# Retention of two batches in halves of 64 tokens, every product 64 by 64 by 64

## The chip, the core and the metric

The kernel runs on one core of a Trainium2 chip. The core has TensorE (PE, matrix products; loads of its stationary operand are listed as PEld), VectorE (DVE), ScalarE (ACT), GpSimd (POOL) and SyncE (SP), which issues all DMAs here. PE reads SBUF and writes PSUM, a memory of eight banks of 512 float32 per partition. The metric is the time of one execution on the device in microseconds (us), lower being better.

## The reference, cut to what matters

```python
# q, k, v: (4 batches, 8 heads, 576 tokens, 64), float32
scores = q @ k^T / 8
D[i, j] = gamma_h ** (i - j) if i >= j else 0,   gamma_h = 1 - 2 ** (-5 - h)
ret    = (scores * D) @ v                         # retention: causal, decaying by head
x      = ret with the heads side by side          # (2304 tokens, 512)
h      = ((x @ w1) * (x @ w2)) @ w3 @ w_out       # first block
y      = h @ w_in;  g = max(y, 0) + alpha * min(y, 0);  out = g @ w_out2
```

The retention can be computed by chunks of tokens: within a chunk by scores times decay times v, and against all earlier tokens by a state, the decayed sum of k^T v (64 by 64 per head).

## The kernel before, in words

All of it is one program without loops on the chip; Python writes the instructions out. The order on PE, ScalarE and SyncE is that in which they are written; VectorE's and GpSimd's instructions are placed by a scheduler, which chooses among the ready ones, and each of the two then follows its fixed list.

The retention handles two heads at a time as a pair (four pairs per batch): one head on partitions 0 to 63, one on 64 to 127. The class Retention (line 371) cuts a batch into four chunks of 128 tokens and a tail of 64. Its products, per chunk and pair:

- scores (line 400): k^T q, contraction over 64, output 128 by 128, one product per head, into the tile sc (two banks, one buffer). VectorE multiplies sc by the decay mask into rt (line 423).
- values (line 451): state times q (line 467, 64 by 64, moving 128 tokens) and v times rt (line 476, contraction over 128), both summed in the tile o (one buffer in the batches of this change). ScalarE rounds o to the high half xh of x, VectorE takes the rest as xl (lines 181 and 182, called by parts).
- moments (line 427): k^T v of the chunk (line 434, contraction over 128, output 64 by 64) into st (one buffer). VectorE adds them to the aged state: S (line 442, line 440 in the first chunk); GpSimd multiplies S by gamma ** 128: aged (line 446).

A step (line 496) writes the scores of chunk c + 1, the values of chunk c and the moments of chunk c + 1, so a batch has six steps, c = -1 to 4. What VectorE and ScalarE have to do is put off through the list `later` and written at the next flush.

In the third and fourth batch (crossed, line 363) the heads of odd pairs are swapped between the partition halves, so that state products use all four 64 by 64 quadrants of the PE array; cross (line 516) reloads parts of the constants for it by 16 small DMAs.

Between the steps stands the first block: ab_unit (line 621) writes two groups of 12 products of 128 by 128 by 512 (gemm3, line 188, float32 split in two halves) and after each group calls a function that flushes and, at a given rate, runs the next step. In the third batch a step comes after every second group (rate 7/15), in the fourth mostly after each (rate 7/9). VectorE and ScalarE also prepare weights there: lines 93 to 122 turn the bits of 64-bit weights into float32 (a, b), lines 271 to 309 build sums of them (t, wo2u).

Of the kernel before, what the change touches and what calls it, by code (L numbers as in the profile page):

```python
# [7 lines left out]
F32 = mybir.dt.float32  # L8
# [138 lines left out]
def retention_moe_kernel(ctx: ExitStack, tc, qk, kv, w_out1, w3t, w12, w_in, w_out2, alpha, c_row, c_pair, out):  # L147
# [79 lines left out]
    class Operands:  # L227
# [4 lines left out]
        def __init__(self, rooms, small=None, stays=None):  # L232
            self.rooms, self.small, self.stays, self.turn = rooms, small, stays, 0
            self.w = Weights(nc, None, room, 0)
            for c in range(C2):
                self.w.add(w_out2[c], None)
            self.calls, self.u = {}, {}
            self.now = 0
# [11 lines left out]
        def places(self, j, u):  # L250
            ops = self.PLACES[u]
            if j == self.stays:
                return [wop[4 * WOPS.index(op) + 3][:, 1].rearrange("p (h w) -> p h w", h=2) for op in ops]
            n = len(ops)
            if n == 1 and self.small:
                t = self.small.tile([P, 512], F32R, tag="u1", name=f"wo2{u}_{j}")
            else:
                t = self.tile(f"wo2{u}_{j}").bitcast(F32R)[:, 0:512 * n]
            return t.rearrange("p (n h w) -> p n h w", n=n, h=2)
# [83 lines left out]
    abp = pool(pb, "abp", side="right")  # L343
    per_pair = decay.tile([P, NPAIR, 3 * CH + 64], F32, name="per_pair")
    mask = per_pair[:, :, 0:2 * CH].rearrange("p n (h i) -> p h n i", h=2)
    mtail = per_pair[:, :, 2 * CH:2 * CH + 64]
    qs = per_pair[:, :, 2 * CH + 64:]
    per_row = decay.tile([P, 128], F32, name="per_row")[:, 0:H + NPAIR]
# [22 lines left out]
    class Retention:  # L371
# [28 lines left out]
        def scores(self, c):  # L400
            b, n = self.b, self.n
            sc = self.psum["sc"].tile([P, 2, 512], F32, tag="sc", name=f"sc{b}_{c}")
            q, k = qt[b], kt[b]
            if c == NCH - 1:
                rt = self.rt[c] = attn.tile([P, NPAIR, 64], F32, tag="rte", name=f"rte{b}")[:, 0:n]
                for m, p in enumerate(self.pairs):
                    for rows, _, _ in places(b, p):
                        nc.tensor.matmul(sc[rows, 0, m * 64:(m + 1) * 64], k[p][rows, 512:S],
                                         q[p][rows, 512:S],
                                         start=True, stop=True, skip_group_check=True)  # L410
                later.append(lambda: nc.vector.tensor_tensor(
                    out=rt, in0=sc[:, 0, 0:64 * n].rearrange("p (n i) -> p n i", n=n), in1=mtail[:, self.ps],
                    op=ALU.mult))
                return
            i0 = c * CH
            rt = self.rt[c] = attn.tile([P, 2, NPAIR, CH], F32, tag="rt", name=f"rt{b}_{c}", bufs=2)[:, :, 0:n]
            for m, p in enumerate(self.pairs):
                for rows, _, r in places(b, p):
                    nc.tensor.matmul(sc[:, r, m * CH:(m + 1) * CH], k[p][rows, i0:i0 + CH],  # L419
                                     q[p][rows, i0:i0 + CH],  # L420
                                     start=True, stop=True, skip_group_check=True)

            later.append(lambda: nc.vector.tensor_tensor(
                out=rt, in0=sc[:, :, 0:n * CH].rearrange("p h (n i) -> p h n i", n=n), in1=mask[:, :, self.ps],
                op=ALU.mult))
# [70 lines left out]
        def steps(self):  # L496
# [9 lines left out]
                return run  # L506
            return [step(c) for c in range(-1, NCH)]

    qt, kt, kvt, vt = ({b: {} for b in range(B)} for _ in range(4))

    def in_places(b, p, t, src):

        for rows, pp, _ in places(b, p):
            nc.sync.dma_start(out=t[rows], in_=src[pp])  # L514

    def cross():

        for p in range(1, NPAIR, 2):
            in_places(2, p, gc[:, p:p + 1], c_row[:, H + p:H + p + 1])
            for h in range(2):  # L520
                nc.sync.dma_start(out=mask[:, h, p], in_=c_pair[:, p, (1 - h) * CH:(2 - h) * CH])
            in_places(2, p, mtail[:, p], c_pair[:, p, 2 * CH:2 * CH + 64])
            in_places(2, p, qs[:, p], c_pair[:, p, 2 * CH + 64:])

    def load_pair(b, p):
        x = attn.tile([P, 2, S], F32, tag=f"qk{p}", name=f"qk{b}_{p}")
# [143 lines left out]
        return run  # L670

    def retention(b):
        r = Retention(b, list(range(NPAIR)), psum1)
        left = [p for p in range(NPAIR) if (b, p) not in prepared]

        def prep():
            r.scale(left)
            r.prep(left)

        return Steps([prep] + r.steps())  # L680
# [369 lines left out]
    class Group:  # L1050
# [6 lines left out]
        def product(self, ps, a, b, fresh=True):  # L1057
            a, b = operand(self.j, a), xop[self.p, b]
            n = 0
            for k in range(2):  # L1060
                ks = slice(k * P, (k + 1) * P)
                for x, y in ((0, 0), (0, 1), (1, 0)):
                    nc.tensor.matmul(ps, a[:, x, ks], b[:, y, k], start=(fresh and n == 0), stop=(n == 5),  # L1063
                                     skip_group_check=True)
                    n += 1
# [424 lines left out]
```

## Time and profile before

| | |
|---|---|
| median of three runs | 782.3 us (779.87 to 785.56) |
| the profiled execution | 783.55 us, of which its span 781.7 us |
| PE busy | 768.9 us (98%), 4928 records of products |
| DVE busy | 587.3 us (75%) |
| ACT busy | 380.4 us (49%) |
| POOL busy | 63.8 us (8%) |
| mean granted clock of PE | 0.997 of full speed |

Times in the profile count from the start of the span. "Busy" joins overlapping instructions; products on PE are pipelined and their ends modelled, so the starts say more than the durations. A float32 product appears as two records, each with its weight load.

### The profile page before, as it was taken

The numbers are of one execution on the slowest core, as the hardware profiler recorded it, in microseconds if no ns is written. First come the engines' busy times: TensorE is split into PE (matmuls) and PEld (weight loads), VectorE is DVE, ScalarE is ACT, GpSimd is POOL, SyncE is SP. The second block draws the span as 40 slices with busy tenths as digits, with TensorE's granted clock in tenths as the row PEclk, the third lists the DMA queues.
The fourth block names the chain that finished last, engine by engine and source line by source line (L and its number), as shares of the span: only waits on it lengthen the run. The fifth ranks groups of instructions, "written<-read, shape, count | busy, mean of one in ns | idle before, by whom it ended". The sixth has DMA issues, their size and how long they took to land.

```text
span 781.7 us, 13197 instructions
## 1 busy us (share of the span) xinstructions
PE 768.9 (98%) x4928; PEld 688.9 (88%) x4928; DVE 587.3 (75%) x951; ACT 380.4 (49%) x665; POOL 63.8 (8%) x73
## 2 busy tenths in 40 slices
PE   8999999998999999999999999999999999999998
PEld 5788788887788988899999999999999888888887
DVE  4894889569857779688974768778767877777874
ACT  3643474334445466464654546546534444444442
POOL 4410400051000000000000200110200000000000
PEclk9999999999999999999999999999999999999999
DMA  9943965798576667799993796564899754444440
GB/s 353 358 160 105 340 246 202 239 287 259 212 249 204 189 197 256 248 327 368 407 375 138 262 362 225 172 228 154 286 339 366 234 152 128 140 126 136 135 128 28
DMA packets 116225, 182.11 MB, mean 233 GB/s; under 512 B 9920, under 2 KB 82624, under 8 KB 116160
## 3 DMA queue, kind: packets, MB, share of 16 engines
q1 hardware_dynamic: 116160, 181.26, 68.1%
q8 instruction: 39, 0.64, 0.4%
q14 instruction: 26, 0.21, 0.1%
HBM read 117.00 MB, written 64.23 MB: 232 GB/s over the span
## 4 chain that ended last, share of the span: by engine, by line
PE 83%; DVE 7%; DMA 5%; issue 2%; SPq 2%; ACT 1%; POOL 0%; DVEq 0%; ACTq 0%; POOLq 0%
PE h L1063 21%; PE ps L188 19%; PE y L1007 13%; PE o L1208 12%; PE o L1210 6%; PE pw L822 6%; DMA abd<-ab 2%; PE sc L419 2%; PE o L476 2%; DMA cells<-gd 2%; DVE cells L1189 2%; PE o L467 1%; SPq L514 1%; PE st L434 1%; DVE a L108 1%
## 5 line engine op out<-in xcount | busy, mean ns | idle before, releaser
L188 PE MATMUL ps<-xh,w 128*128 128x512 f32 (+1 forms) x640 | 186.1, 372 | 1.8 <-ACT f L651 1.8
L188 PEld LDWEIGHTS ps<-xh,w 128*128 128x128 f32 x640 | 116.1, 188 | 23.3 <-ACT f L651 2.2
L1208 PE MATMUL o<-wop,cells 128*128 128x512 f32 x504 | 126.4, 393 | 0.9 <-DVE cells L1220 0.9
L188 PE MATMUL ps<-xl,w 128*128 128x512 f32 (+1 forms) x320 | 118.0, 369 | 0.0
L1208 PEld LDWEIGHTS o<-wop,cells 128*128 128x128 f32 x504 | 90.8, 189 | 17.7 <-issue 1.4
L1007 PE MATMUL y<-yab,wp 128*128 128x384 f32 x576 | 100.0, 334 | 0.0
L1007 PEld LDWEIGHTS y<-yab,wp 128*128 128x128 f32 x576 | 99.9, 188 | 0.1
L1189 DVE TENSOR_TENSOR cells<-cells,cells 128x1024 fp32r<-128x1024 f32 x63 | 76.4, 1222 | 25.7 <-ACT cells L1183 25.6
L1210 PEld LDWEIGHTS o<-wop,cells 128*128 128x128 f32 x504 | 68.7, 190 | 4.9
L1210 PE MATMUL o<-wop,cells 128*128 128x256 f32 x504 | 70.2, 282 | 0.0
L188 PEld LDWEIGHTS ps<-xl,w 128*128 128x128 f32 x320 | 60.4, 189 | 9.5
L1183 ACT CAST cells<-cells 128x1024 fp32r<-128x1024 f32 x63 | 64.9, 1054 | 7.0 <-DVE cells L1176 4.6
L108 DVE CUSTOM_DVE_ANT_0 a<-a,b 128x1024 uint16<-128x1024 uint16 x72 | 53.2, 738 | 2.9
L1063 PE MATMUL h<-xT,wu 128*128 128x384 f32 x288 | 54.7, 334 | 0.2 <-DVE g L1082 0.2
L1063 PE MATMUL h<-xT,wv 128*128 128x384 f32 x288 | 54.9, 335 | 0.0
L1076 DVE SCALAR_TENSOR_TENSOR g<-h,al,g 128x384 f32<-128x384 f32 x48 | 29.4, 614 | 32.6 <-ACT g L1075 29.5
L637 ACT CAST ab<-f 128x512 fp32r<-128x512 f32 (+1 forms) x40 | 23.1, 577 | 61.2 <-DVE f L641 51.8
L1063 PEld LDWEIGHTS h<-xT,wu 128*128 128x128 f32 x288 | 50.3, 188 | 0.5 <-DVE g L1082 0.5
L1063 PEld LDWEIGHTS h<-xT,wv 128*128 128x128 f32 x288 | 50.3, 188 | 0.3 <-DVE g L1082 0.3
L103 DVE TENSOR_SCALAR a<-a 128x512 f32<-128x512 f32 x72 | 31.9, 443 | 22.9 <-ACT a L93 22.5
L822 PE MATMUL pw<-wo,w 128*128 128x512 f32 x192 | 43.7, 389 | 0.0
L822 PEld LDWEIGHTS pw<-wo,w 128*128 128x128 f32 x192 | 36.0, 188 | 7.4
(130 smaller groups left out, 1139.4 us busy)
## 6 DMA issues: line engine op xcount, KB each, us to landing
gd<-g SPq DMA_DIRECT2D x96, 192.0 KB, 4.4
cells<-gd SPq DMA_DIRECT2D x36, 512.0 KB, 6.3
abd<-ab SPq DMA_DIRECT2D x32, 512.0 KB, 5.2
wod<-wo2u SPq DMA_DIRECT2D x49, 256.0 KB, 4.0
wop<-wod SPq DMA_DIRECT2D x21, 512.0 KB, 6.5
yab<-abd SPq DMA_DIRECT2D x24, 384.0 KB, 8.0
raw<-in_w_dram SPq DMA_DIRECT2D x16, 512.0 KB, 8.0
rawo<-in_w_out_dram SPq DMA_DIRECT2D x16, 512.0 KB, 5.2
```

The source lines that it names most:

```text
L103: nc.vector.tensor_scalar(out=a, in0=a, scalar1=self.LEAST, scalar2=self.MOST, op0=ALU.max, op1=ALU.min)
L108: nc.vector.tensor_tensor(out=a.bitcast(I32), in0=a.bitcast(I32), in1=b, op=ALU.add)
L188: nc.tensor.matmul(ps, a, bb, start=(n == 0), stop=(n == last))
L637: nc.scalar.copy(t[:, 0], f)
L822: nc.tensor.matmul(acc[i], a[:, ic], bb, start=(k == 0 and n == 0), stop=(k == C1 - 1 and n == 2))
L1007: nc.tensor.matmul(ys[o], wpc[c][a][:, oc], yab[b, c][:, bb], start=(c == 0 and i == 0), stop=(c == C1 - 1 and i == 2))
L1063: nc.tensor.matmul(ps, a[:, x, ks], b[:, y, k], start=(fresh and n == 0), stop=(n == 5), skip_group_check=True)
L1076: nc.vector.scalar_tensor_tensor(out=g, in0=ps, scalar=sal[:, c], in1=g, op0=ALU.mult, op1=ALU.max)
L1183: nc.scalar.copy(h.bitcast(F32R), self.q[name])
L1189: nc.vector.tensor_tensor(out=l.bitcast(F32R), in0=q[name], in1=h, op=ALU.subtract)
L1208: nc.tensor.matmul(ps, h[:, k], w[k], start=(fresh and k == 0), stop=(k == C1 - 1), skip_group_check=True)
L1210: nc.tensor.matmul(ps[:, 256:], l[:, k], w[k][:, 0:256], start=False, stop=(k == C1 - 1), skip_group_check=True)
```

## The change

A class Halves takes the place of Retention in the crossed batches. A chunk still has 128 tokens, but its products are of one shape: contraction over 64, 64 columns of output partitions, 64 moving tokens. For scores, only the two diagonal blocks of 64 tokens are made; the decay within a chunk from its first to its second half goes through the state: moments are taken per half, `half` (line 573 or 575) is the state after the first half, S the state after the second. The moments of the first half lie in bank 0 of the tile sc, those of the second in st. A value tile gets v times rt by halves, then, behind a drain of PE, the reads of S for the first 64 tokens and of half for the second, in two groups by the heads' places; the moments (or the tail's scores) of the next chunk are written ahead of each drain. The first 64 rows of the key decay (kd) are replaced by a copy from the mask, and the constants are reloaded in the places that the halves need. In excerpt:

```diff
+    class Halves(Retention):
...
+        def scores(self, c):
...
+            for m, p in enumerate(self.pairs):
+                for rows, _, r in places(b, p):
+                    for h in range(2):
+                        i0 = c * CH + 64 * h
+                        nc.tensor.matmul(sc[HEADS[h], r, m * 64:(m + 1) * 64], k[p][rows, i0:i0 + 64],
+                                         q[p][rows, i0:i0 + 64],
+                                         start=True, stop=True, skip_group_check=True)
+            later.append(lambda: nc.vector.tensor_tensor(
+                out=rt, in0=sc[:, :, 0:64 * n].rearrange("p r (n i) -> p r n i", n=n), in1=mask2[:, :, self.ps],
+                op=ALU.mult))
...
+        def moments(self, c):
...
+            st = [self.sc[:, 0, 256:256 + 64 * n]]
+            st.append(self.psum["st"].tile([P, NPAIR, D], F32, tag="st", name=f"st{b}_{c}")
+                      .rearrange("p n d -> p (n d)")[:, 0:64 * n])
+            def share(m, p):
+                x = None
+                for j, (rows, _, _) in enumerate(places(b, p)):
+                    for h in range(2):
+                        y = nc.tensor.matmul(at[h][rows, m * 64:(m + 1) * 64], v[p][HEADS[h], 4 * j + c],
+                                             v[p][HEADS[h], 8 + 4 * j + c],
+                                             start=True, stop=True, skip_group_check=True)
...
+            def halfway():
+                new = self.half[c] = attn.tile([P, NPAIR, D], F32, tag="half", name=f"half{b}_{c}", bufs=3)[:, 0:n]
+                if c == 0:
+                    nc.vector.tensor_copy(new, st[0])
+                else:
+                    nc.vector.tensor_tensor(out=new, in0=self.state[c], in1=st[0], op=ALU.add)
+                aged = attn.tile([P, NPAIR, D], F32, tag="aged", name=f"aged{b}_{c}", bufs=2)[:, 0:n]
+                nc.gpsimd.tensor_tensor(out=aged, in0=new, in1=gc[:, self.ps].unsqueeze(2)
+                                        .to_broadcast([P, n, D]), op=ALU.mult)
+                def state():
+                    s = self.state[c + 1] = attn.tile([P, NPAIR, D], F32, tag="S", name=f"S{b}_{c}",
+                                                      bufs=3)[:, 0:n]
+                    nc.vector.tensor_tensor(out=s, in0=aged, in1=st[1], op=ALU.add)
+                later.append(state)
+            later.append(halfway)
...
+        def values(self, c, between):
...
+            for m, p in pairs:
+                for h in range(2):
+                    for j, (_, pp, r) in enumerate(places(b, p)):
+                        product(h, pp, m, v[p][HEADS[h], 8 + 4 * j + c], rt[HEADS[h], r, m], False)
+            kinds = 2 if crossed(b) else 1
+            for kind in range(kinds):
+                for x in between[n // kinds * kind:n // kinds * (kind + 1)]:
+                    x()
+                nc.tensor.drain()
+                for h in range(2):
+                    for m, p in pairs:
+                        if kinds == 1 or (p + h) % 2 == kind:
+                            read(m, p, h)
...
+        def steps(self):
+            def step(c):
+                def run():
+                    flush()
+                    if c == NCH - 1:
+                        self.tail_values(c)
+                        return
+                    between = self.scores(c + 1) or self.moments(c + 1)
+                    if c >= 0:
+                        self.values(c, between)
...
     def cross():
+        first_half = HEADS[0]
+        nc.vector.tensor_copy(kd[first_half].rearrange("p (n h) -> p n h", h=2),
+                              mask[first_half, :, :, CH - 1].rearrange("p h n -> p n h"))
...
-        r = Retention(b, list(range(NPAIR)), psum1)
+        r = (Halves if crossed(b) else Retention)(b, list(range(NPAIR)), psum1)
```

How the order moves, at three places. The first is PE in step c = 1 of the third batch (names carry batch and chunk; two equal rows joined as x2, x4). Before, 32 products of four shapes:

```order
L419 MATMUL sc2_2_1446<-qk2_0_916 128x128 x2
L419 MATMUL sc2_2_1446<-qk2_1_938 128x128 x2
...
L467 MATMUL o2_1_1456<-qk2_0_916,S2_0_1312 64x128 x2
L467 MATMUL o2_1_1456<-qk2_1_938,S2_0_1312 64x128 x2
...
L476 MATMUL o2_1_1456<-rt2_1_1351,kv2_0_917 64x128 x2
...
L434 MATMUL st2_2_1473<-kv2_0_917 64x64 x2
```

and now 64 products of one shape:

```order
L541 MATMUL sc2_2_1501<-qk2_0_917 64x64 x4
...
L617 MATMUL o2_1_1520<-rt2_1_1370,kv2_0_918 64x64 x4
...
L562 MATMUL sc2_2_1501<-kv2_0_918 64x64
L562 MATMUL st2_2_1519<-kv2_0_918 64x64
...
L617 MATMUL o2_1_1520<-qk2_0_917,S2_0_1364 64x64 x2
L617 MATMUL o2_1_1520<-qk2_2_963,S2_0_1364 64x64 x2
L617 MATMUL o2_1_1520<-qk2_1_939,half2_1_1467 64x64 x2
L617 MATMUL o2_1_1520<-qk2_3_992,half2_1_1467 64x64 x2
L562 MATMUL sc2_2_1501<-kv2_2_964 64x64
...
L617 MATMUL o2_1_1520<-qk2_1_939,S2_0_1364 64x64 x2
```

The reads of the state (S, half) have moved from ahead of the products with rt to behind them, in two groups between the moments; a drain, which the order does not list, stands ahead of each group.

The second place is VectorE at the first chunk of the fourth batch (a6, a7 are weights being prepared). Before:

```order
L275 TENSOR_TENSOR wo2u4_2_2023<-t3_2_1981,wo2u4_2_2023 128x2x256
L103 TENSOR_SCALAR a6_2028<-a6_2028 128x512
L423 TENSOR_TENSOR rt3_0_2005<-sc3_0_2004,per_pair_101 128x1024
L104 TENSOR_SCALAR a6_2028<-a6_2028 128x512
L440 COPY S3_0_2057<-st3_0_2014 128x256
```

and now:

```order
L275 TENSOR_TENSOR wo2u4_2_2186<-t3_2_2128,wo2u4_2_2186 128x2x256
L103 TENSOR_SCALAR a6_2191<-a6_2191 128x512
L104 TENSOR_SCALAR a6_2191<-a6_2191 128x512
L545 TENSOR_TENSOR rt3_0_2152<-sc3_0_2151,per_pair_101 128x8x64
L573 COPY half3_0_2220<-sc3_0_2151 128x256
L103 TENSOR_SCALAR a7_2195<-a7_2195 128x512
L106 SCALAR_TENSOR_TENSOR a6_2191<-rawo6_2092,a6_2191 128x512
L104 TENSOR_SCALAR a7_2195<-a7_2195 128x512
L583 TENSOR_TENSOR S3_0_2225<-aged3_0_2222,st3_0_2169 128x256
```

L104 has moved ahead of rt, half follows rt, and S, which now needs the aged half, comes four places later.

The third place is VectorE ahead of step c = 3 of the fourth batch, where the last xl of step 2 (two pieces, since a block of x ends within the chunk) frees the output tile. Before:

```order
L275 TENSOR_TENSOR wo2u4_3_2259<-t3_3_2194,wo2u4_3_2259 128x2x256
L103 TENSOR_SCALAR a8_2264<-a8_2264 128x512
L423 TENSOR_TENSOR rt3_3_2224<-sc3_3_2223,per_pair_101 128x1024
L104 TENSOR_SCALAR a8_2264<-a8_2264 128x512
L103 TENSOR_SCALAR a9_2268<-a9_2268 128x512
L106 SCALAR_TENSOR_TENSOR a8_2264<-rawo8_2132,a8_2264 128x512
L104 TENSOR_SCALAR a9_2268<-a9_2268 128x512
L182 TENSOR_TENSOR xl3_1704<-o3_2_2233,xh3_1703 128x4x64
L442 TENSOR_TENSOR S3_3_2297<-aged3_2_2218,st3_3_2250 128x256
L108 ISA a8_2264<-a8_2264,b8_2265 128x1024
L106 SCALAR_TENSOR_TENSOR a9_2268<-rawo9_2134,a9_2268 128x512
L182 TENSOR_TENSOR xl4_2294<-o3_2_2233,xh4_2293 128x4x64
```

and now:

```order
L275 TENSOR_TENSOR wo2u4_3_2530<-t3_3_2429,wo2u4_3_2530 128x2x256
L103 TENSOR_SCALAR a8_2535<-a8_2535 128x512
...
L106 SCALAR_TENSOR_TENSOR a9_2539<-rawo9_2333,a9_2539 128x512
L545 TENSOR_TENSOR rt3_3_2461<-sc3_3_2460,per_pair_101 128x8x64
L575 TENSOR_TENSOR half3_3_2562<-S3_2_2458,sc3_3_2460 128x256
L309 TENSOR_SCALAR a8_2535<-a8_2535,al_71 128x512
L108 ISA a9_2539<-a9_2539,b9_2540 128x1024
L182 TENSOR_TENSOR xl3_1851<-o3_2_2479,xh3_1850 128x4x64
L290 TENSOR_TENSOR t1_4_2674<-a8_2535 128x256
L583 TENSOR_TENSOR S3_3_2573<-aged3_3_2564,st3_3_2478 128x256
L309 TENSOR_SCALAR a9_2539<-a9_2539,al_71 128x512
L182 TENSOR_TENSOR xl4_2569<-o3_2_2479,xh4_2568 128x4x64
```

The five rows left out here are L104, L103, L106, L104 and L108 of a8 and a9. All the preparation of a8 and a9 up to L106 now stands ahead of rt, and 15 instructions instead of 10 lie between wo2u4 and the last xl.

## Rows read from the trace of the kernel before

**Rows 1.** Page, part 1: busy time, share of the span, instructions.

```profile
PE 768.9 (98%) x4928; PEld 688.9 (88%) x4928; DVE 587.3 (75%) x951; ACT 380.4 (49%) x665; POOL 63.8 (8%) x73
```

**Rows 2.** Stretches: length, busy of PE, PEld, DVE, ACT, POOL (instructions), clock, DMA, GB/s.

```profile
175.50:211.40 35.90, 32.77 (x361) 26.51 (x360) 32.72 (x64) 15.64 (x30) 3.72 (x4) 0.95 0.68 236
182.70:186.81 4.11, 4.11 (x48) 3.82 (x48) 4.11 (x10) 0.62 (x1) 2.20 (x1) 0.60 0.98 385
211.40:781.70 570.30, 565.40 (x3189) 527.36 (x3182) 427.00 (x663) 284.82 (x481) 17.09 (x18) 1.00 0.67 226
```

**Rows 3.** Waits of PE, whole span: us in total, times, longest us.

```profile
PE sc L419 <- DVE rt L423: 2.4, 1, 2.4
PE o L467 <- DVE xl L182: 0.6, 1, 0.6
```

**Rows 4.** Chain of waits, third batch: start us, us, what; between them the steps.

```profile
95.34 11.17 PE ps L188 x48
...
108.22 5.69 PE ps L188 x24
...
116.49 5.69 PE ps L188 x24
...
125.35 5.66 PE ps L188 x24
...
134.19 5.66 PE ps L188 x24
...
141.93 5.67 PE ps L188 x24
...
148.22 16.56 PE ps L188 x72
```

**Rows 5.** Timeline of PE in 147.847 to 147.86, last step: start us, us, instruction.

```profile
147.63 0.35 PE L467 MATMUL o<-qk,S 64*64 64x64 f32 x12
147.81 0.24 PE L476 MATMUL o<-rte,kv 64*64 64x64 f32 x4
```

**Rows 6.** Timeline of PE, step c = 3 of the third batch.

```profile
140.19 0.33 PE L467 MATMUL o<-qk,S 64*64 64x128 f32 x2
140.24 0.22 PE L408 MATMUL sc<-qk 64*64 64x64 f32 x2
```

**Rows 7.** Timeline of all engines at the first chunks of the fourth batch.

```profile
181.10 0.42 DVE L103 TENSOR_SCALAR a<-a 128x512 f32<-128x512 f32 x1
181.43 1.21 DVE L423 TENSOR_TENSOR rt<-sc,per_pair 128x1024 f32<-128x1024 f32 x1
...
182.70 2.08 PE L419 MATMUL sc<-qk 64*128 64x128 f32 x16 [2.38 <-DVE rt L423]
...
183.46 2.20 POOL L446 TENSOR_TENSOR aged<-S,per_row 128x256 f32<-128x256 f32 x1 [7.84 <-DVE S L440]
...
186.81 0.50 PE L188 MATMUL ps<-xh,w 128*128 128x512 f32 x1
```

**Rows 8.** Timeline of PE and DVE, steps c = 2 and 3 of the fourth batch.

```profile
198.60 1.16 PE L419 MATMUL sc<-qk 64*128 64x128 f32 x16
...
199.89 0.69 DVE L275 TENSOR_TENSOR wo2u<-t,wo2u 128x512 fp32r<-128x512 f32 x1 [2.12 <-ACT wo2u L271]
200.50 0.42 DVE L103 TENSOR_SCALAR a<-a 128x512 f32<-128x512 f32 x1
...
205.44 0.42 DVE L182 TENSOR_TENSOR xl<-o,xh 128x256 fp32r<-128x256 f32 x1
205.77 0.49 DVE L309 TENSOR_SCALAR a<-a,al 128x512 f32<-128x512 f32 x1
...
206.01 0.67 PE L467 MATMUL o<-qk,S 64*64 64x128 f32 x16 [0.61 <-DVE xl L182]
...
207.63 0.50 PE L188 MATMUL ps<-xh,w 128*128 128x512 f32 x1
```

**Rows 9.** Timeline of SyncE, reloading of the constants ahead of the third batch.

```profile
64.74 2.39 SPq L514 DMA_DIRECT2D per_pair<-const_pair_dram  x4
```

More of the change, by code (lines that the diff above doesn't have):

```diff
@@ L345, in retention_moe_kernel @@
     mask = per_pair[:, :, 0:2 * CH].rearrange("p n (h i) -> p h n i", h=2)
+    mask2 = per_pair[:, :, 0:CH].rearrange("p n (h i) -> p h n i", h=2)
     mtail = per_pair[:, :, 2 * CH:2 * CH + 64]
@@ L516, in cross @@
     def cross():
+        first_half = HEADS[0]
+        nc.vector.tensor_copy(kd[first_half].rearrange("p (n h) -> p n h", h=2),
+                              mask[first_half, :, :, CH - 1].rearrange("p h n -> p n h"))
+        odd = slice(1, NPAIR, 2)
+        for h, rows in enumerate(HEADS):
+            i0 = 64 * h
+            for p in range(0, NPAIR, 2):
+                nc.sync.dma_start(out=per_pair[rows, p, 0:CH].rearrange("p (r i) -> p r i", r=2),
+                                  in_=c_pair[rows, p, 0:2 * CH].rearrange("p (r i) -> p r i", r=2)[:, :, i0:i0 + 64])
+            for r in range(2):
+                at = (1 - r) * CH + i0
+                nc.sync.dma_start(out=per_pair[rows, odd, 64 * r:64 * r + 64], in_=c_pair[rows, odd, at:at + 64])
+        in_places(2, 1, mtail[:, odd], c_pair[:, odd, 2 * CH:2 * CH + 64])
+        in_places(2, 1, qs[:, odd], c_pair[:, odd, 2 * CH + 64:])
         for p in range(1, NPAIR, 2):
             in_places(2, p, gc[:, p:p + 1], c_row[:, H + p:H + p + 1])
[L520 to L523, printed above, removed]
     def load_pair(b, p):
```

77 lines of the change are left out of this document (added).

## The prediction

> **What bounds the kernel now.** I read the page first: TensorE (PE) is busy 98% of the span [rows 1], so the first question for any edit is what it does on PE. Then two stretches: in 175.50 to 211.40, where the fourth batch runs, PE is busy 32.77 of 35.90 us and the granted clock averages 0.95; after it PE is busy 565.40 of 570.30 us [rows 2], so a microsecond won or lost by PE before 211 reaches the end nearly whole. The waits of PE name what makes it idle there: 2.4 us for the decayed scores (rt) and 0.6 us for xl, the low half of an output [rows 3]. Then the chain of waits through batch three: it is PE alone, and the holes between its stretches of L188 are the six steps of the retention [rows 4]: 1.71, 2.58, 3.17, 3.18, 2.08 and 0.62 us (the first begins at 95.34 + 11.17 = 106.51), 13.34 us in all. Batch four has the same products plus its stalls.
>
> **The products.** A float32 product leaves two records on PE. A batch had 288 records in its six steps (32, 48, 64, 64, 48, 32); with every product cut into 64 by 64 by 64 it has 544 (64, 112, 128, 128, 80, 32), as the loops give it: per 128 tokens and pair four products instead of two in scores, in the products with v, in the moments and in the reads of the state, but none more in the last step of 64 tokens. What a 64 by 64 by 64 record costs, the last step shows, where all four quadrants of the array are in turn: 12 records from 147.63 to 147.81, 0.18 us [rows 5], so a round of four takes 0.06. That step's 32 records are 8 rounds, 0.48 of its 0.62 us; 0.14 is entering and leaving.
>
> The new products go round the four quadrants too, except the reads, which come as four products on two quadrants and then four on the other two, and the last scores, on two. PE fills idle quadrants from further down its list: two records of L467 start at 140.19, before the last two of L408 at 140.24 [rows 6]. So I add one round per group of reads and two for the last scores: 16, 30, 34, 34, 24 and 8 rounds.
>
> **The drains.** Steps of 128 tokens now contain two nc.tensor.drain() each, 8 in a batch; no row of these stages shows one. Lower bound: one round, 0.06 us, if the list just goes on. Upper bound from rows: a record lasts 0.22 [rows 6], and PE follows a releaser after 0.06 (rt ends at 181.43 + 1.21 = 182.64, PE starts at 182.70 [rows 7]) to 0.15 (xl ends at 205.44 + 0.42 = 205.86, PE starts at 206.01 [rows 8]): 0.37. An end of a record and a short release are nearest to what a drain says: 0.22 + 0.06 + 0.02 for a refilled array, **0.30**.
>
> Steps of batch three, changed: 0.14 + 16 x 0.06 = 1.10; 0.14 + 1.80 + 0.60 = 2.54; 0.14 + 2.04 + 0.60 = 2.78 twice; 0.14 + 1.44 + 0.60 = 2.18; 0.62. Sum 12.00 against 13.34: **1.3 us gained** (3.3 with drains of 0.06, 0.8 with 0.37). I look for a new wait in it: per chunk VectorE had rt of 1.21 [rows 7] and a narrow S, 0.33, and has rt at half the width, about 0.60, with half and S at 0.33 each, hardly other work in all: 1.54 before, 1.26 now; 24 matmuls of L188 (5.7 us) lie between two steps, and by the order the xl that the next step waits for stays ahead of it. None. GpSimd's fourth ageing per batch has the same cover.
>
> **Batch four, first two steps.** Only 12 matmuls lie between steps (5.66 / 2 = 2.83 us) and VectorE is late. The gain of the first step (0.6) only lets PE wait earlier. In step 0 PE waits for the single buffer of scores. It was free when rt had read it, at 182.64. Now the first half's moments lie in the same buffer, and half must have read it too; and the order puts the second shift (L104) ahead of rt. From L103 at 181.10 [rows 7]: L104 needs its result, 0.42 + 0.04; rt 0.33 later, at 181.90; half 0.60 later, at 182.50; it ends at 182.92 and PE goes on at 182.98 instead of 182.70, +0.28. The wait grows from 2.4 to some 3.2 us. The step took 4.11 us (to 186.81 [rows 7]) where batch three needs 2.58, since after its 2.4 us of idleness PE was granted 0.60 on average, most of it the lower level of 1.2 GHz [rows 2]: 1.5 us lost, which I leave as it is. The second half's moments need S of the first chunk, which now comes behind half and GpSimd's ageing (it took 2.20 us here [rows 7]): S is ready between 184.2 and 185.6, PE needs it at about 184.9, 0 to 0.7, take 0.25. Sum: **0.5 later**. Steps 1 and 2 gain 0.39 each as in batch three: **0.8 earlier**.
>
> **Batch four, step 3.** Here lies the largest term. The outputs have one buffer; the products of step 3 wait for the last xl of step 2. Before, 10 instructions stand on VectorE between wo2u4 (199.89) and that xl; PE starts on the outputs at 206.01, 0.61 late. The new order puts 15 there (the parts of the last weights go ahead of rt, half and xl), and the wait now stands ahead of the step's scores too. By spacing in the rows [rows 8]: a 512-wide instruction 0.61 (199.89 to 200.50), a narrow one 0.33 (205.44 to 205.77), L309 0.49 less the same overlap of 0.09. From wo2u4: six wide ones 3.66, a dependent L103 0.46, seven narrow ones 2.31, two L309 0.80, the last xl 0.42: 7.65. It ends at 207.54 instead of 205.86, and PE starts 0.15 later, at 207.69. wo2u4 itself waits for ScalarE's cast behind the L188 products ahead of step 2, so its distance from step 2 stays. From there the step has 2.18 us to go, against 207.63 - 206.01 = 1.62: it ends at 209.87, **2.2 later**. PE will have idled from about 204.2 (198.60 + 2.78 + 2.83) to 207.7, 3.5 us, more than the 2.4 us after which the clock was lower; a lower clock again costs between 0 and 1.5, take **1.0**.
>
> **The rest.** SyncE issues 16 small transfers where it issued 16, at about 0.6 us each [rows 9], before and behind the same neighbours: nothing, at most 0.5 either way. VectorE's one copy of 64 by 8 at the start of batch two: under 0.2, beside PE's products.
>
> **Sum.** -1.3 + 0.5 - 0.8 + 2.2 + 1.0 = +1.6 us. The profiled execution took 783.55 us, so 785.15; it lies 1.25 above the median of 782.3, so against the median **783.9 us**.
>
> One rule of the Trainium skill speaks against the change. The rows give 15 ns from record to record over 12 records [rows 5], and none shows more than 32 such records in a row. "TensorE: Matmul & The Clock Gate", section "Wait — 56ns, not 53.3ns?", states a floor of about 25 ns from start to start however small a matmul is, and 62 ns if each goes through the sequencer's code. By the floor alone 544 records would be an estimated 13.6 us before any drain, and a batch would lose instead of gain; the rows contradict it over the length they show.
>
> **Rivals.**
> 1. *Drains are cheap and the clock stays up* (faster). Place: 14 drains that count (8 in batch three, 6 in batch four behind its first wait). Below 0.18 us each the sum turns negative: 1.6 - 14 x 0.12 = -0.1. At 0.06 it is 1.6 - 14 x 0.24 = -1.8, and without the second fall of the clock -2.8: 779.5. For it: between the two kinds of products of the last step PE shows no pause [rows 5]; against it: PE is told to empty. 22%.
> 2. *PE cannot sustain the small records* (slower). If a long run of 64 or more goes at 25 ns, half of the 50 at which the 64 records of a step go now (3.17 / 64 [rows 4]), because the list is fed no faster, batch three costs 544 x 0.010 = 5.4 more, batch four 4.8 more after its first wait (480 records): 783.9 + 10.2 = 794. It decides from 18 ns on (544 x 0.003 = 1.6 us a batch). For it: four instructions per product, twice as many products; against it: 12 records at 15 ns, steadily. The same rise comes if a drain costs 0.9. 9%.
> 3. *The wait of step 3 moves the fourth batch further* (slower): VectorE waits for GpSimd's ageing at each S, and the wait repeats in step 4, with the clock down in both: another 3 to 5 us, 787 to 789. For it: the ageing of 2.20 [rows 7]; against it: VectorE has less to do in each step, and ahead of wo2u4 it stood idle for 2.12 us [rows 8]. 14%.
> 4. *The change is not what it says*: the two quadrants of the reads are not filled ahead; 28 rounds a batch rather than 8 extra: 20 x 0.06 = 1.2 us more each, 786.3. Inside my range; 10%.
>
> My forecast as worked out, 782 to 786: 45%.
>
> **Numbers.** A measurement of this kernel can tell about 1% from no change (7.8 us); the runs before lie between 779.87 and 785.56. The range takes in rivals 1, 3 and 4 and the bounds of the drain, and the scatter of a median: 778.5 to 789.5. Faster by over 1% would be under 774.5, more than all gains together: 3%. Slower by over 1% is above 790.1, rival 2 and the end of rival 3: 11%. Within 1%: 86%.
>
> **What would show it.** In the changed profile: the holes between the stretches of L188 in batch three at 1.1, 2.5, 2.8, 2.8, 2.2 and 0.6 us; gaps of 0.3 ahead of the reads, at a record named DRAIN; PE's longest waits 3.2 us for half (L573) and about 3.4 us for xl ahead of step 3 of batch four, the granted clock below 1 in both. I am wrong if PE's small records stand 20 ns or more apart within a group, if VectorE's xl of step 2 does not end some 7.7 us after wo2u4, or if a stretch after 212 gains idle time.

## The result and the profile after

The changed kernel takes 791.2 us, median of 4 runs (789.8 to 794.6), against 782.2 before: the ratio is 1.0126, 95% interval 1.0095 to 1.0156. It is slower by 1.3%; 783.9 was forecast, and 789.5 was the top of the range. The profiled execution took 792.2 us (span 790.4, against 781.7 before). Three executions among all runs of this document took 1.5 to 2.7 ms for no reason that is known and are left out of its medians and ratios.

Part 1 of the page of the changed kernel, as [rows 1], and three views of its trace. The stretches first (columns as in [rows 2]); the first is the fourth batch and the second all that follows, as there:

```profile
PE 769.5 (97%) x5440; PEld 688.1 (87%) x5440; DVE 588.1 (74%) x960; ACT 379.7 (48%) x665; POOL 68.2 (9%) x75
```

```profile
175.50:218.57 43.07, 34.71 (x616) 27.75 (x606) 32.73 (x68) 15.37 (x30) 3.70 (x5) 0.80 0.57 203
218.57:790.40 571.83, 565.65 (x3189) 527.04 (x3182) 426.59 (x663) 284.22 (x482) 17.09 (x18) 1.00 0.67 225
...
182.00:192.00 10.00, 8.69 (x122) 7.37 (x123) 10.00 (x22) 2.06 (x4) 1.66 (x2) 0.50 0.68 236
192.25:209.00 16.75, 14.17 (x295) 11.03 (x293) 10.92 (x22) 6.47 (x12) 1.82 (x2) 1.00 0.53 200
209.25:215.75 6.50, 4.92 (x84) 4.18 (x85) 4.87 (x12) 1.65 (x4) 0.00 (x0) 0.50 0.24 94
```

The fourth batch is 43.07 us long where it was 35.90: 7.2 of the 8.7 us that the span grew lie here. The clock there is 0.80 on average where it was 0.95. The lower three rows say when: 1.2 GHz for 10 us and again for 6.5, where the kernel before was low once, for some 3.4. The rest of the kernel is 1.5 us longer.

PE's waits (us in total, times, longest us), as [rows 3]:

```profile
PE sc L541 <- DVE half L573: 3.7, 1, 3.7
PE o L617 <- DVE xl L182: 3.6, 1, 3.6
...
PE o L617 <- issue: 1.5, 7, 0.5
...
PE pw L1000 <- ACT w L114: 1.4, 1, 1.4
```

The two forecast waits are there, the first half a microsecond longer. Two lines are new: PE stops seven times at reads of the state with no releaser (most of them 0.16 us, behind a drain, and one of 0.5), and much later, at 326 us, it waits for a weight.

The chain of waits through the third batch, as [rows 4] (the holes between the stretches of L188 are the six steps):

```profile
95.11 11.19 PE ps L188 x48
107.45 5.71 PE ps L188 x24
115.89 5.66 PE ps L188 x24
124.34 5.67 PE ps L188 x24
133.65 5.67 PE ps L188 x24
141.56 5.71 PE ps L188 x24
147.89 16.56 PE ps L188 x72
```

1.15, 2.73, 2.79, 3.64, 2.24 and 0.62 us, 13.17 in all, where 13.34 stood before and 12.00 was forecast. Five holes are within 0.2 of the forecast; step c = 2, the fourth hole, is 0.86 too long. The timeline of PE in steps c = 1 and c = 2 (start us, us, instruction, idle before it and its releaser; line 617 is the products that give the outputs):

```profile
121.48 0.69 PE L541 MATMUL sc<-qk 64*64 64x64 f32 x32
...
131.11 0.23 PE L562 MATMUL st<-kv 64*64 64x64 f32 x2
131.45 0.27 PE L617 MATMUL o<-qk,S 64*64 64x64 f32 x2
...
132.57 0.22 PE L617 MATMUL o<-qk,half 64*64 64x64 f32 x1
133.32 0.33 PE L617 MATMUL o<-qk,half 64*64 64x64 f32 x2 [0.53 <-issue]
```

The first row is 32 records of scores in 0.69 us: less the 0.22 of the last one, 31 starts are 0.47 us, 0.015 each. The next two are a drain: 0.34 from start to start instead of 0.015, so 0.32 us, against 0.30 forecast. The last two are something else: with two records of the step still to come, PE stands for half a microsecond and waits for nothing that the profile shows.

Last, the timeline of PE and VectorE at the two waits, as [rows 7, 8]:

```profile
181.08 0.41 DVE L103 TENSOR_SCALAR a<-a 128x512 f32<-128x512 f32 x1
...
183.03 1.13 PE L541 MATMUL sc<-qk 64*64 64x64 f32 x32 [3.67 <-DVE half L573]
...
187.68 0.79 PE L188 MATMUL ps<-xh,w 128*128 128x512 f32 x1
...
202.44 0.69 DVE L275 TENSOR_TENSOR wo2u<-t,wo2u 128x512 fp32r<-128x512 f32 x1 [2.12 <-ACT wo2u L271]
...
210.05 0.41 DVE L182 TENSOR_TENSOR xl<-o,xh 128x256 fp32r<-128x256 f32 x1
...
210.61 1.13 PE L617 MATMUL o<-rt,kv 64*64 64x64 f32 x32 [3.64 <-DVE xl L182]
...
214.16 0.79 PE L188 MATMUL ps<-xh,w 128*128 128x512 f32 x1
```

PE goes on at 183.03 (182.98 forecast); from wo2u4 to the end of the last xl are 8.02 us (7.65 forecast). But step 0 takes 4.65 us and step 3 takes 3.55, at half the clock. The first 12 of the 24 products of L188 behind step 0 take 4.88 us from start to start, where they took 2.85.

### The profile page after: what moved, and what is told of

Same layout as the page of the kernel before. It is cut to its first block, busy times and chain, and to the rows that moved or that the text cites. A ratio compares the mean times of both kernels' runs of the same rounds, so it can differ in the third digit from the quotient of the medians.

```text
span 790.4 us, 14261 instructions
## 1 busy us (share of the span) xinstructions
PE 769.5 (97%) x5440; PEld 688.1 (87%) x5440; DVE 588.1 (74%) x960; ACT 379.7 (48%) x665; POOL 68.2 (9%) x75
## 4 chain that ended last, share of the span: by engine, by line
PE 81%; DMA 7%; DVE 6%; issue 2%; ACT 2%; SPq 0%; POOL 0%; ACTq 0%; POOLq 0%
PE h L1241 22%; PE ps L188 18%; PE o L1386 14%; PE y L1185 13%; PE o L1388 7%; DMA abd<-ab 5%; PE o L617 2%; DVE a L106 1%; DMA qk<-in_qk_dram 1%; PE o L477 1%; DVE a L108 1%; PE sc L420 1%; PE o L468 1%; DVE a L103 1%; DMA raw<-in_w_out_dram 1%
## 5 line engine op out<-in xcount | busy, mean ns | idle before, releaser
L188 PE MATMUL ps<-xh,w 128*128 128x512 f32 (+1 forms) x640 | 188.4, 375 | 1.8 <-ACT f L829 1.8
L188 PEld LDWEIGHTS ps<-xh,w 128*128 128x128 f32 x640 | 117.4, 191 | 23.9 <-ACT f L829 2.2
L188 PE MATMUL ps<-xl,w 128*128 128x512 f32 (+1 forms) x320 | 118.9, 372 | 0.0
L188 PEld LDWEIGHTS ps<-xl,w 128*128 128x128 f32 x320 | 61.2, 191 | 9.7
L108 DVE CUSTOM_DVE_ANT_0 a<-a,b 128x1024 uint16<-128x1024 uint16 x72 | 52.0, 723 | 2.9
L103 DVE TENSOR_SCALAR a<-a 128x512 f32<-128x512 f32 x72 | 33.6, 467 | 23.4 <-ACT a L93 22.8
```

Of the source, the lines that this page charges most:

```text
L103: nc.vector.tensor_scalar(out=a, in0=a, scalar1=self.LEAST, scalar2=self.MOST, op0=ALU.max, op1=ALU.min)
L108: nc.vector.tensor_tensor(out=a.bitcast(I32), in0=a.bitcast(I32), in1=b, op=ALU.add)
L188: nc.tensor.matmul(ps, a, bb, start=(n == 0), stop=(n == last))
```

## The experiments

Theory A was that the loss is the fourth batch's: two waits of PE for VectorE, and the lower clock behind them. Theory B, its rival, was that the halves cost by themselves, in any batch. "Against before" is always the ratio to runs of the kernel before on the same chip.

**Which batch.** third_only and fourth_only use halves in one batch and reload the other layout between the batches; third_clean and fourth_clean keep both layouts.

```
-        r = (Halves if crossed(b) else Retention)(b, ...)
+        r = (Halves if b == 2 else Retention)(b, ...)     # fourth_only, fourth_clean: b == 3
+    kd from c_row, masks of 128 reloaded behind batch 3   # third_only; fourth_only: masks of halves
+    halved, kd2 = tiles of their own, 8 transfers more at the head of cross()   # the two clean ones
```

> Only the third batch in halves of 64; the fourth as before, for which 12 small transfers bring the masks of 128 and the old decays back behind the third batch. Theory A (the loss arises in the fourth batch alone: its two waits of PE for VectorE, of 3.67 and 3.64 us, and the lower clock behind them): 782.3 us +- 1, the six steps of the third batch 13.2 us in all as in the changed kernel (13.3 before), PE's waits for rt of 2.4 and for xl of 0.6 us back. Theory B (twice as many small products and the drains cost by themselves, in whichever batch): half of the loss, about 786.5. A stall of 0.5 us in step 3 of the third batch is there again if the list of instructions is fed too slowly, and gone if it was chance.

> Only the fourth batch in halves of 64; the third as before, 8 small transfers bring the masks of halves between them. Theory A: the whole loss, 791 +- 1.5, with the waits for half and xl near 3.7 us each and the granted clock at 0.50 for 10 and 7 us. Theory B: about 786.5.

> Only the third batch in halves, with masks and decays of its own (2.5 KB a partition, loaded at the start of the stage with the others), so that nothing is reloaded ahead of the fourth batch, which is as before, VectorE's order included. Theory A (the loss is the fourth batch's): 781.5 +- 1, the third batch's six steps 13.0 to 13.3 us against 13.34. Theory B (halves cost by themselves in either batch): 785 or more.

> Only the fourth batch in halves, in the same way. Theory A: the whole loss, 790.5 +- 1.5, with two waits for VectorE of some 3.5 us and the lower clock behind them. Theory B: 785 to 787.

third_only took 786.5 us (1.0058, 1.0036 to 1.0080), fourth_only 795.4 (1.0167, 1.0129 to 1.0205), third_clean 790.5 (1.0108, 1.0065 to 1.0151), fourth_clean 797.4 (1.0189, 1.0151 to 1.0227). By the totals third_only (786.5) and third_clean ("785 or more") came out as theory B had it, and the two with halves in the fourth batch alone lie above what either theory had. But in each pair the two losses together exceed the whole: the transfers that I added cost more than what I wanted to see. Where it went is read by setting the n-th product of L188 of a kernel beside the n-th of the kernel before. third_only: 0.4 us won over the third batch, 3.8 lost from 173 to 191; its six transfers of masks stand on SyncE from 171 to 178. third_clean is 9.3 us late when its third batch begins: 2.4 arose by 40 us, ahead of the transfers; 4.2 are the longer wait in this row of its waits, and 2.7 came behind it, at a granted clock of 0.50:

```profile
PE ps L188 <- ACT f L836: 6.0, 1, 6.0
```

The wait is 5.6 in fourth_clean and 1.8 in the kernel before (0.3 to 2.8 in the profiles of kernels with 16 transfers there). Inside the batches the halves' third loses between -0.4 (third_only) and +0.5 us (third_clean, with a stop of 0.79 in it), and the halves' fourth, from 173 to 216, loses 7.5 (changed kernel), 8.0 (fourth_clean) and 11.3 (fourth_only, whose eight transfers stand there). This reading by stages is for theory A; the totals are not, and can't decide.

**The transfers.** To see whether it was they, the kernel before with fewer:

```
+        odd = slice(1, NPAIR, 2)            # both odd pairs in one transfer; mtail and qs in one
+        in_places(2, 1, gc[:, odd], ...); mask[:, h, odd]; in_places(2, 1, per_pair[:, odd, 2 * CH:], ...)
```

> The kernel before with its 16 small transfers ahead of the third batch joined to 6 of the same bytes. Two kernels with 8 transfers more there waited 5.6 to 6.0 us instead of 1.8 for ScalarE's f at 93 us and lost 4.0 to 6.6 us up to 98. If a small transfer there costs SyncE 0.6 us on the path, the wait goes, 1.8 us less up to 98, of which batch four's wait for rt takes back some: 780 to 781.5 in the end. If those kernels lost by something else, the wait stays at 1.8 and the time at 782.

779.4 us, ratio 0.9978 (0.9960 to 0.9997). The wait for f is no longer in its list of waits. Ten transfers fewer make the kernel faster by a little more than the uncertainty, so such transfers do lie on the path there. My "nothing, at most 0.5 either way" held only since the change has 16 of them as before.

**The clock.** Does PE's wait or what follows it decide how long the clock stays low? rt_twice computes half of rt of chunk 0 twice; two_drains and rt_twice_drains put drains into that step; keep_busy, before_busy and wide_first put products nobody reads ahead of a step or behind its scores. keep_busy and wide_first are edits of the changed kernel, the other four of the kernel before.

```
+            if (b, c) == (3, 0):             # rt_twice
+                later.append(rt[:, 0] = sc[:, 0] * mask[:, 0] once more)
+                    if (self.b, c) == (3, 0):
+                        nc.tensor.drain()    # two_drains, rt_twice_drains: behind scores, behind values
+                        self.busy(self.o, 34)  # keep_busy: ahead of scores; and (3, 3): self.busy(self.sc, 26)
+                        self.busy(self.o, 18)  # wide_first: behind scores
+                        8 products into o      # before_busy: ahead of scores
```

> The kernel before, with half of the decayed scores of chunk 0 of the fourth batch computed a second time, so that the scores' buffer is free later and PE's wait of 2.4 us grows to about 4.1, with the large products of before behind it. Theory C1 (how long PE idled sets how long the clock stays low afterwards): the clock stays at 0.50 for some 9 us after PE goes on, as in the changed kernel, 1.7 + 3 us or more lost, 787 and up. Theory C2 (what PE runs afterwards sets it: small products and drains keep it low): the clock rises 3.3 us after PE goes on as before, only the 1.7 us of wait lost, 784.0.

> The kernel before with two drains put on PE in step 0 of the fourth batch, one behind the scores and one behind the outputs, where PE goes on after its wait of 2.4 us. In the kernels with products of 128 the granted clock stood at 0.50 for 3.4 us (before, with the third batch alone in halves, and with the longer wait of rt_twice), in those with halves for 10.2 us. If the short stops at the drains keep the clock down: 6 us or more at 0.50 here and the step over 4.9 us. If it is the small products: 3.4 us at 0.50 as before, and the step 4.1 plus two drains, 4.7 to 4.9 us.

> The kernel of rt_twice (products of 128, PE's wait ahead of step 0 of the fourth batch drawn out to some 4 us) with two drains in that step, one behind the scores and one behind the outputs. In rt_twice the clock fell and stood at 0.50 for 3.4 us. If the short stops at the drains keep it down, 6 us or more at 0.50 here; if it is the small products of the halves that do, 3.4 us again.

> The changed kernel with products of 128 by 128 by 256 whose results nobody reads, put on PE ahead of steps 0 (34 of them) and 3 (26) of the fourth batch, into space of the outputs and the scores that nobody uses there; VectorE's order is the changed kernel's. Theory A1 (the clock falls because PE idles; PE's time after it is lost to the clock): the granted clock stays 1.00 from 176 to 216 or nearly, step 0 takes 2.75 us instead of 4.65, the 12 products behind it 2.85 instead of 4.88, step 3 about 2.2 instead of 3.55, 0.6 less behind it: 5.9 us less than the changed kernel, 785.3. Theory A2 (the small products with their drains hold the clock down whatever ran ahead of them): the clock falls all the same, 790 or more. The waits for VectorE stay in both.

> The kernel before with 8 such products (1 us) in its wait of 2.4 us ahead of step 0 of the fourth batch: the clock stays at 1.00, and the 1.5 us that step 0 lost at the lower clock are won: 780.0. If the stop of 1.4 us that is left suffices for the clock to fall, 781.5.

> The changed kernel with 18 products of 128 by 128 by 256 that nobody reads behind the scores of step 0 of the fourth batch, that is behind PE's first wait (3.7 us at the lower clock). If it is the small products that keep the clock down, it stands at 0.50 for some 3.4 us instead of 10.2, and PE's loss is those 3.7 us alone. If the longer wait itself does it, 10 us at 0.50 again.

rt_twice: 784.0 us (1.0033, 1.0017 to 1.0048), as C2 had it. PE waited 4.4 us, longer than in the changed kernel, and the clock was low for some 3.4 us as before; this row of its stretches lies in that time:

```profile
186.00:189.00 3.00, 3.00 (x37) 2.78 (x34) 3.00 (x5) 0.62 (x1) 0.00 (x0) 0.50 0.40 153
```

two_drains (786.3, one run) says nothing: it came late to the step, PE waited 1.5 us only and the clock did not fall there. rt_twice_drains (783.9, one run) repeats it with a wait of 3.2; both drains are in the step, PE's two pauses are seen, and again the clock is low for 3.25 us:

```profile
184.75:188.00 3.25, 3.14 (x32) 2.54 (x27) 3.25 (x6) 1.14 (x3) 0.00 (x0) 0.50 0.15 53
```

So in one profile each, neither a longer wait nor drains kept the clock down longer. Over all the profiles, in slices of a quarter of a microsecond and without the end of the kernel, the clock was low 27 times. In 12 of these spells PE ran 64 by 64 by 64 products: eleven last 6.5 to 13.5 us, one 3.25. In the other 15 it ran larger ones only: eleven last 3 to 3.25 us, and four 6.5 to 6.75 (before_gap, below, where PE stopped twice, and fourth_clean, third_clean and two_drains at 96 to 101 us). This row lies in the one of two_drains, which holds the end of a single stop of 2.7 us:

```profile
95.75:102.50 6.75, 6.19 (x15) 4.83 (x16) 5.24 (x9) 4.92 (x10) 0.00 (x0) 0.50 1.03 420
```

Behind stops of 3.2 to 4.4 us, all eight spells with 64 by 64 products are long and all four without them are short. That is a strong tendency of the small products and no rule.

keep_busy: 789.0 us (1.0108, 1.0076 to 1.0140), against 785.3 forecast. Its profiled execution did what A1 says: clock 1.00 throughout and 785.7 us:

```profile
175.50:215.00 39.50, 36.81 (x649) 30.66 (x640) 32.93 (x68) 16.50 (x32) 4.30 (x5) 1.00 0.60 216
```

Its other runs took 788.4 to 792.6, one of them (789.6) also with a mean granted clock of 1.000, and no profile shows where; the 60 products are there whether PE would wait or not, so a PE that comes late is not let off its wait. before_busy: 782.2 (1.0015, 0.9993 to 1.0036), no gain over the kernel before, though its profiled execution took 780.4 with the clock at 1.00. wide_first (784.0, one run) could not answer its question: PE waited only 1.9 us for half in it and the clock never fell. That makes it the nearest to a changed kernel without lower clock: 1 to 2 us above the kernel before, of which its 18 products alone are 2.3 us of PE's time. But it is one run.

**VectorE's order.** in_turn, turn6 and gap_turn5 have VectorE's instructions in written order (from the fourth batch's stretch, its step 2, its step 1); the gap kernels move the place with 24 products between steps ahead of step 0; turn6_busy adds 18 products ahead of step 0.

```
+        if c == 6:                           # turn6; 5: gap_turn5; ahead of the loop: in_turn
+            in_turn.enter_context(tc.manual_schedule(engines={mybir.EngineType.DVE}))
-            run = loading(also(cycle(r if c else None, 7 / 9)))
+    turns = [0, 1, 1, 0, 1, 1, 1, 1, 1, 0]   # *_gap, gap_turn5; 7 / 9 gives 0, 1, 1, 1, 0, 1, 1, 1, 1, 0
```

> The changed kernel, with VectorE's instructions of the stretch that holds the fourth batch in the order in which they are written, not placed by the scheduler: of the 15 that stood between wo2u4 and the last xl ahead of step 3, five or so now stand behind it. Theory A: the wait ahead of step 3 is gone, and with it its 3.6 us, 1.35 of step 3 at the lower clock and 0.6 behind it, 5.6 in all; the wait ahead of step 0 (some 3.7 us) and the 10 us of lower clock behind it stay: 785.5. If VectorE's order is not what the second wait hangs on, 790 or more.

> As in_turn, and the one place where 24 products of L188 lie between two steps of the fourth batch is moved from behind step 0 to ahead of it. Theory A: PE comes to step 0 2.8 us later, waits about 0.9 us instead of 3.7, and the granted clock stays at 1.00 throughout; step 1, with 12 products ahead of it, waits some 1.1 for half. Against the changed kernel 5.6 + 2.8 + 1.9 + 2.0 - 1.1 = 11.2 less: 780. Theory B (halves cost by themselves): not under 784.

> The kernel before with that place moved in the same way, its VectorE order by the scheduler. PE's wait of 2.4 us for rt and the lower clock behind it (1.5) go, but rt of chunk 1 ends 8.5 us after rt of chunk 0 by VectorE's rows and PE has only 5.4 us of work between: a wait of some 2.7 us ahead of step 1 takes its place, with the clock down again. 782 +- 1.5; if VectorE had the time, 778.5.

> The changed kernel, with VectorE's instructions in the order in which they are written from step 2 of the fourth batch on, and the scheduler's order up to there: between wo2u4 and the last xl ahead of step 3 stand 9 instructions instead of 15. Theory A: the first wait and the 10 us of lower clock behind it stay, the wait ahead of step 3 (3.6 us) and its lower clock go: 5.6 us less than the changed kernel, 785.5. If the second wait only moves to another place, 789 or more.

> As turn6, and 18 products that nobody reads (2.2 us) on PE in its first wait, ahead of step 0 of the fourth batch. The wait ends when it ended, but PE idles less than 1.8 us at a stretch. Theory A1: the clock stays at 1.00, and another 3.9 us (1.9 of step 0 and 2.0 of the 12 products behind it) are won: 781.5, level with the kernel before. If the small products hold the clock down by themselves, as turn6.

> The changed kernel with the 24 products of L188 between two steps of the fourth batch ahead of step 0 instead of behind it, and VectorE in written order from step 1 on; up to there the scheduler's order. Theory A: the wait ahead of step 0 shrinks from 3.7 to some 0.9 us, one of about 1.4 comes ahead of step 1, none ahead of step 3, and the clock stays at 1.00: 780 to 781.5, level with the kernel before or a little under it. Theory B (halves cost by themselves): 785 or more.

in_turn: 793.7 us (1.0153, 1.0110 to 1.0196). The second wait went down to 1.0, nearly gone as expected, but written order made VectorE stop 1.4 us for one of ScalarE's pieces ahead of rt, and the first wait grew:

```profile
PE sc L541 <- DVE half L573: 6.9, 1, 6.9
...
PE o L617 <- DVE xl L182: 1.0, 1, 1.0
```

in_turn_gap: 791.5 (1.0132, 1.0097 to 1.0167), waits of 4.4 for half and 2.4 for S. before_gap: 781.7 (1.0003, 0.9986 to 1.0020), as forecast: the wait of 2.4 became one of 2.6 a step later. turn6: 789.0 (1.0106, 1.0084 to 1.0129); the wait ahead of step 3 fell from 3.6 to 1.3 and its spell of lower clock is gone, yet by the ratios the kernel is some 1.6 us better instead of 5.6, which is within the uncertainty; the profiled execution, 786.9, is the fastest of its four runs. turn6_busy: 790.8 (1.0109, 1.0088 to 1.0131), no better. Its trace shows a stop in the reads of step 1 (timeline of PE, and the DMA queues in 197.00 to 199.50: packets, MB, share of 16 engines):

```profile
196.41 0.35 PE L621 MATMUL o<-qk,S 64*64 64x64 f32 x6
200.29 0.45 PE L621 MATMUL o<-qk,half 64*64 64x64 f32 x7 [3.54 <-issue]
```

```profile
q1 hardware_dynamic: 412, 1.00, 101.6%
q8 instruction: 1, 0.02, 2.2%
```

PE stands still for 3.5 us; in that time the data queue is full and one load of instructions is under way.

gap_turn5: 787.6 (1.0091, 1.0074 to 1.0109). Both waits for VectorE are gone (a new one of 0.8 us stands ahead of the last step), but the time is not 780; it is what theory B had:

```profile
PE o L617 <- issue: 1.8, 7, 0.9
PE ps L188 <- issue: 1.8, 1, 1.8
...
PE sc L562 <- POOL kv L386: 1.2, 1, 1.2
```

Two stops without a releaser, 0.9 in the third batch and 1.8 in the fourth, the clock at 0.50 for 3.25 us behind the second, and a wait for GpSimd in step -1 with another 3.25. So theory A as I had it is not enough: without the waits three quarters of the ratio stay. Nor is the lower clock what is left: two of the five runs had a mean granted clock of 1.000 and took 788.4 and 787.1.

**The list of instructions.** In eight of the ten profiles so far with halves in the third batch, PE stopped at one and the same place: the last two records of step c = 2 start 0.27 to 1.10 us behind the record before them, where their neighbours stand 0.015 to 0.06 apart. In wide_first and turn6 it did not.

```
-                nc.tensor.matmul(warm, idle[:, 0:P], idle[:, :512], ...)
+                for m in range(2): nc.tensor.matmul(warm[:, 0:256], idle[:, 0:P], idle[:, :256], ...)
```

> The changed kernel with each of the 26 warming products at the start of the kernel, and of the few beside the first steps, cut into two of half the width: PE's work in time is the same, its list some 30 to 60 instructions longer ahead of the third batch. In the changed kernel and three of its variants PE stalled 0.5 to 0.9 us at one place, ahead of the last products of step 3 of the third batch, with no releaser. If that is the list of instructions arriving late in pieces of fixed size, the stall is now 15 to 60 instructions earlier in the list, inside the same step or at its start; if it is something in the step itself, it stays where it was.

The last reads of steps c = 1 and c = 2 in its chain of waits (in the changed kernel 0.48 and, with the stop, 1.33 us):

```profile
123.63 0.76 PE o L617 x16
...
132.37 0.48 PE o L617 x16
```

With the list longer ahead of it, the stop is not there; step c = 2 takes 2.79 us instead of 3.64, and the step ahead of it 3.07 instead of 2.79, so 0.3 of it is now earlier. The third batch takes 12.60 us. The number of instruction loads on queue q8 in the third batch is 2 before and 5 in the changed kernel. Both are what a list that arrives in pieces would give, and that the delay turned up elsewhere speaks against a cause inside the step. But two kernels without the shift lack the stop too, so this one profile supports the theory and does not settle it. (791.0, one run: the fourth batch had both spells of the lower clock, 6.75 us each.)

## Why the prediction was wrong

What bounds the kernel, the drain (0.32 against 0.30), the small products without one (15 ns apart, now over 32 records) and the wait ahead of step 3 (3.64 against "from about 204.2 to 207.7, 3.5 us") were right. The floor of 25 ns that the Trainium skill states in "TensorE: Matmul & The Clock Gate", section "Wait — 56ns, not 53.3ns?", does not hold in these runs: 15 ns over 32 records. The resume of step 0 (0.05 off) agrees partly by luck: 182.98 was worked out without the 1.3 us that the same sum takes off ahead of it. PE came to batch four 0.33 us earlier than before, and VectorE's L103 stands at 181.08 instead of 181.10. Against the sum of +1.6, the profiles show +8.7:

- *The products and the drains*, -1.3: measured -0.2 over the third batch (13.17 against 13.34). Of the 1.2 that are missing, 0.86 are step c = 2, with the stop in it, and 0.2 step c = 0. turn6 and wide_first, without the stop, gain 0.9 over the six steps; in the eight profiles with it the batch lies between 0.6 won and 0.5 lost. So the stop is some 0.8 of the missing 1.2. If late instructions cause it, rival 2 had the mechanism, "the list is fed no faster", but as 25 ns for every record; it came as one stop in a batch. The rows of the kernel before show no such stop; its list is loaded less often.
- *Batch four, first two steps*, +0.5: measured +3.2: 2.0 in the first 12 products behind step 0 (4.88 against 2.85), 0.7 since PE, which came 0.33 earlier, goes on 0.33 later than before, and 0.5 in the step itself (4.65 against 4.11). The failed step is "1.5 us lost, which I leave as it is". The clock stayed at 1.2 GHz for 10 us instead of 3.4.
- *Batch four, step 3*, +2.2 and +1.0: measured +5.0. 2.2 of it is the longer wait and the step's own work; the lower clock and its 6.5 us cost 2.0 and not 1.0. The last 0.7: the xl ended 8.02 us behind wo2u4 and not 7.65, and wo2u4 came 2.55 us later than before, where PE behind step 2 was 2.18 late. wo2u4 hangs on the products ahead of step 2, so what step 2 gains only lets PE wait earlier; the sum counted that 0.4 as won.
- *Steps 1 and 2*, -0.8: measured -0.7.
- *The rest*, 0: measured +1.5. The stream of weights that ScalarE and VectorE unpack from 216 on started as much later as PE, then fell back another 2.9 us (between 262 and 284 of the kernel before), which no row explains, and at 326 PE waited 1.4 for it. "A stretch after 212 gains idle time" was named as what would make me wrong.

The sum is -0.2 + 3.2 - 0.7 + 5.0 + 1.5 = 8.8, within rounding of 8.7. So the waits themselves were nearly right, and what comes behind a wait was too small in three terms. Of the rivals that I gave a time, 3 (787 to 789) came nearest; its mechanism (GpSimd's ageing at each S) was not the one.

Open: gap_turn5, without either wait, still is 0.91% slower (0.74 to 1.09), and its profile accounts for 2.7 us of stops and the clock behind them in one execution. That profile lies 3.3 us above the one of the kernel before, while the medians on its chip lie 7.1 apart (787.6 and 780.5), so much of the remainder is in no profile. That late instructions are this remainder is argued, not shown. Nor was the drain taken away, so what the halves cost without it is not known. And why the clock mostly stays low for longer over 64 by 64 products is open; one profile each speaks against drains and longer waits as the reason.

## What to carry over

Price a stall of PE with what runs behind it: behind the wait of 3.7 us, step 0 took 1.9 us more than the same step of the third batch (4.65 against 2.73), and the 12 products after it 2.0 more. Cutting a product into four multiplies instructions, and their loads (five instead of two in the third batch) run beside the data's, so count records per microsecond as well as the time of one. When an experiment moves transfers to another place, price them first: two of mine were drowned by eight small ones.

## What was not expected of the hardware

- The clock after a stop: low for 3 to 3.25 us with larger products only (eleven spells of 15), for 6.5 to 13.5 with 64 by 64 by 64 products (eleven of 12).
- The clock fell in the kernel before after 2.4 us without work and in in_turn after 1.9 (at 96 us), but not after 1.5 (two_drains), 1.9 (wide_first) and 2.7 (six_transfers), so the length of the stop alone does not tell.
- PE stopped with nothing to wait for, 0.3 to 3.5 us, with a load of instructions under way beside a full data queue in the longest. That the instructions came late is the likeliest reading; no run settles it.
- Small transfers on SyncE ahead of the third batch: 8 more made PE's wait for f 3.9 and 4.2 us longer, and 1.8 and 2.7 were lost behind it at the lower clock; 10 fewer won 1.7 in the end (0.2 to 3.1 by the interval).
